# LSH attention with a routed MoE on one core: the mask's store split into the exchange, the bits weighted on ScalarE, and a new order of a pair

## The chip, the cores and the metric

The kernel runs on one core of a Trainium2 chip. The metric is the device time of one execution in microseconds. The core has TensorE (PE in the profile, PEld for its weight loads), VectorE (DVE), ScalarE (ACT), GpSimd (POOL) and SyncE (SP), which here only issues DMAs. Every engine works through its own list of instructions in order and waits for the others through semaphores.

## The reference, cut

Four batches of eight heads with 768 positions of 64 numbers. A query sees a key only where six sign bits of their projections agree. What attention gives goes, token by token, to one of eight experts.

```python
q_bits = (np.einsum('bhsd,dk->bhsk', q, proj) > 0)          # 6 bits of every query, and of every key
mask = q_bucket[:, :, :, None] == k_bucket[:, :, None, :]
scores = np.where(mask, scale * np.matmul(q, k.transpose(0, 1, 3, 2)), -1e9)
attn = np.exp(scores - np.max(scores, -1, keepdims=True))
attn = attn / (np.sum(attn, -1, keepdims=True) + 1e-9)
x = (attn @ v) as rows of one token, all heads side by side  # 3072 x 512
expert_idx = np.argmax(x @ w_gate, axis=1)
y = np.maximum(x @ w1[e], 0.0) @ w2[e]                       # e: the token's expert
out = gate_w[:, None] * y
```

## The kernel before, in words

The attention works on **pairs of heads**: 16 pairs (numbered 0 to 15), four to a batch. A pair has two half pairs (384 queries each) and 12 **score units** of 128 queries by 768 keys of one head. For a unit PE multiplies (`S`, lines 303 and 305: q and k are split into high and low parts, and the low rows also carry the bits of the mask), DVE finds the peak (`R`, L313), two small instructions make the factor and the bias of the exponential (`A`, on the engine whose letter follows: L318 with L322 on POOL or with L320 on DVE), and ACT takes the exponential (`X`, L329). PSUM has three tiles for scores ("s") and two ("t") for everything else.

The weights of the first half pair are turned by PE (`T`, L343) and copied out of PSUM by ACT or DVE (`E`, L369 or L367, "a" or "v"). Those of the second half pair (units 6 to 11) are turned in blocks of 32 by DVE (`D`, L383) and put in their place by the **exchange** (`Y`, L392): 16 stores from one SBUF tile to another, issued by SP once the last turn is done, at the beginning of the next pair. PE multiplies them with v there (`B1-`, L403), ACT copies the result (`O`, L408), PE turns it into token rows and gate logits in one product (`K`, the projection, L422), and DVE scales and stores them (`L`, L432).

The bits of the **next** pair are made inside a pair: `G` (L258, PE, two "t" tiles), `H` (signs, L238, ACT), `w` (L271: the first 64 rows are multiplied by a weight for each row, on POOL; then L272 stores them to DRAM, issued by SP), and `z` (L276): POOL issues a gather from DRAM into the rows of q and k that carry the mask. `C` are the casts and subtractions of the next pair's q and k on POOL (L202 to L210). A pair's x (q and k of a head, 768 KB) is loaded two pairs ahead, v one ahead; both are issued by SP. For pair 15, x is loaded as pair 14 begins.

Once in a batch, in the second pair of the next batch (pairs 5, 9 and 13), the **routing** of the finished batch runs in seven steps (`Z`, lines 454 to 486), mostly on DVE and POOL, and after it six **scatters** (`N`, L497) of token rows to `sorted_rows`, issued by POOL. Before that, eight stores of empty rows (`fill`, L144) must have filled `sorted_rows`.

The order is written out by hand: `HEAD` (pair 0), `NEXT` (pair 1), `PLAN` (pairs 2 to 14) and `LAST` (pair 15) are lists of the letters above, read from left to right, and each engine and each queue gets its instructions in that order. A trailing "-" means the pair before. The loads hang on the scores: `before(c)` runs ahead of units 0, 2, 4, ... (r is c within the pair), and issues x at r = 3 and v at r = 4.

## Time and profile before

| | us |
|---|---|
| median of three runs | 771.81 |
| lowest, highest | 770.47, 773.38 |
| the profiled execution | 770.12 |
| its span, first to last instruction | 768.1 |
| PE busy in it | 729.5 (95%) |
| DVE, ACT, POOL busy | 457.8, 404.5, 513.3 |
| mean granted clock of PE | 0.987 |

The pairs fill the span up to about 450 us, the experts the rest. A row of the timeline has its start in us from the start of the span, how long it lasts, engine, line, operation, tiles written and read, how many instructions it merges, and in brackets how long the engine had been idle before it and what ended that. Tile names are given without their numbers, so `w` can be one of several tiles. The granted clock is 1.00 at 2.4 GHz and 0.50 at 1.2 GHz.

### The profile page before, as it was taken

The numbers are of one execution on the slowest core, as the hardware profiler recorded it, in microseconds if no ns is written. First come the engines' busy times: TensorE is split into PE (matmuls) and PEld (weight loads), VectorE is DVE, ScalarE is ACT, GpSimd is POOL, SyncE is SP. The second block draws the span as 40 slices with busy tenths as digits, with TensorE's granted clock in tenths as the row PEclk, the third lists the DMA queues.
The fourth block names the chain that finished last, engine by engine and source line by source line (L and its number), as shares of the span: only waits on it lengthen the run. The fifth ranks groups of instructions, "written<-read, shape, count | busy, mean of one in ns | idle before, by whom it ended". The sixth has DMA issues, their size and how long they took to land.

```text
span 768.1 us, 13633 instructions
## 1 busy us (share of the span) xinstructions
PE 729.5 (95%) x4675; PEld 584.0 (76%) x4675; DVE 457.8 (60%) x861; ACT 404.5 (53%) x815; POOL 513.3 (67%) x800
## 2 busy tenths in 40 slices
PE   7998899899999899989988999999999999999996
PEld 4766577567756766675665688899999999989895
DVE  6759688788778888877878674222545522232221
ACT  5767476577657665674665652443434343434310
POOL 6848677688877787786877364584656656668432
PEclk9999999999999999999999999999999999999999
DMA  5928998658667856966497535663535465545201
GB/s 198 299 74 216 302 296 214 176 174 242 169 191 204 240 144 190 250 162 191 143 242 184 160 104 184 243 216 98 176 133 184 136 118 191 184 137 203 86 10 37
DMA packets 56966, 136.39 MB, mean 178 GB/s; under 512 B 12211, under 2 KB 16051, under 8 KB 56896
## 3 DMA queue, kind: packets, MB, share of 16 engines
q1 hardware_dynamic: 50064, 119.13, 53.5%
q0 software_dynamic: 6688, 16.35, 6.4%
q8 instruction: 38, 0.62, 0.3%
q14 instruction: 32, 0.26, 0.1%
q10 hardware_dynamic: 144, 0.03, 0.0%
HBM read 76.61 MB, written 26.33 MB: 134 GB/s over the span
## 4 chain that ended last, share of the span: by engine, by line
PE 62%; POOL 7%; issue 7%; DVE 6%; ACT 6%; DMA 6%; SPq 5%; POOLq 0%; ACTq 0%; DVEq 0%; another core or an unknown queue 0%
PE s L747 17%; PE t L403 10%; PE s L784 10%; PE s L804 7%; SPq L392 5%; PE s L303 4%; PE t L343 4%; ACT e L329 4%; PE s L305 4%; DVE m L313 3%; DMA masks<-bits 3%; PE t L422 2%; PE t L709 2%; ACT pt L369 1%; DMA xd<-in_qk_dram 1%
## 5 line engine op out<-in xcount | busy, mean ns | idle before, releaser
L329 ACT ACTIVATE e<-s,m 128x768 f32<-128x768 f32 x192 | 190.2, 992 | 115.0 <-POOL m L322 100.3
L313 DVE TENSOR_REDUCE m<-s 128x1 f32<-128x768 f32 x192 | 179.3, 949 | 42.1 <-PE s L305 36.7
L675 POOL TENSOR_TENSOR w<-raw,w 128x512 fp32r<-128x512 f32 x112 | 142.1, 1294 | 45.8 <-ACT w L674 45.2
L403 PE MATMUL t<-pt,vt 128*64 128x384 f32 x768 | 130.9, 490 | 0.0
L747 PE MATMUL s<-xh,w 128*128 128x456 f32 (+6 forms) x672 | 126.8, 346 | 0.0
L747 PEld LDWEIGHTS s<-xh,w 128*128 128x128 f32 x672 | 119.2, 188 | 2.9
L343 PE MATMUL t<-ident,e 128*128 128x128 f32 x648 | 93.8, 280 | 9.9 <-ACT pt L369 7.4
L403 PEld LDWEIGHTS t<-pt,vt 128*64 128x64 f32 x768 | 52.3, 137 | 64.9 <-issue 63.7
L343 PEld LDWEIGHTS t<-ident,e 128*128 128x128 f32 x648 | 74.8, 142 | 25.7 <-ACT pt L369 12.8
L383 DVE STREAM_TRANSPOSE w<-e 128x768 f32<-128x768 f32 x84 | 79.1, 961 | 23.4 <-ACT e L329 23.1
L763 DVE SCALAR_TENSOR_TENSOR hh<-s,hh 128x256 fp32r<-128x256 f32 (+7 forms) x64 | 35.5, 555 | 91.2 <-ACT hh L761 87.0
L784 PE MATMUL s<-hh,w 128*128 128x456 f32 (+3 forms) x384 | 78.7, 358 | 0.0
L369 ACT ACTIVATE pt<-t 128x512 f32<-128x512 f32 (+1 forms) x113 | 65.1, 587 | 14.2 <-PE t L343 13.5
L761 ACT ACTIVATE hh<-s 128x256 fp32r<-128x256 f32 (+7 forms) x64 | 31.4, 490 | 76.8 <-PE s L747 76.8
L784 PEld LDWEIGHTS s<-hh,w 128*128 128x128 f32 x384 | 69.9, 188 | 2.4
L817 POOL DMA_INDIRECT out_dram<-y,ix x26 | 25.9, 996 | 67.6 <-DVE y L815 31.6
L674 ACT ACTIVATE w<-raw 128x512 fp32r<-128x512 f32 x112 | 66.3, 623 | 1.7 <-DMA raw<-in_w_dram 1.7
L303 PE MATMUL s<-w 80*128 80x384 f32 x192 | 58.5, 387 | 8.9 <-ACT e L329 5.5
L318 POOL TENSOR_SCALAR m<-m 128x1 f32<-128x1 f32 x126 | 29.5, 234 | 49.2 <-DVE m L313 38.4
L804 PE MATMUL s<-w,hh 128*128 128x512 f32 (+1 forms) x240 | 58.9, 398 | 0.0
L303 PE MATMUL s<-qk 80*128 80x384 f32 x192 | 56.4, 376 | 1.3 <-ACT e L329 0.6
L715 DVE TENSOR_TENSOR xh<-t,xh 128x456 fp32r<-128x456 f32 (+6 forms) x28 | 16.0, 575 | 64.3 <-ACT xh L714 64.0
(211 smaller groups left out, 1117.4 us busy)
## 6 DMA issues: line engine op xcount, KB each, us to landing
raw<-in_w_dram SPq DMA_DIRECT2D x64, 512.0 KB
pt<-w SPq DMA_DIRECT2D x224, 144.0 KB
xd<-in_qk_dram SPq DMA_DIRECT2D x16, 768.0 KB
w<-in_qk_dram SPq DMA_DIRECT2D x14, 768.0 KB
sorted_rows<-xr SPq DMA_DIRECT2D x8, 1156.0 KB
xg<-sorted_rows SPq DMA_DIRECT2D x25, 289.0 KB
vt<-in_v_dram SPq DMA_DIRECT2D x16, 384.0 KB
masks<-bits SPq DMA_DIRECT2D x15, 192.0 KB
```

The source lines that it names most:

```text
L303: nc.tensor.matmul(p[:, a, :HALF], k[0:80, 2, c], k[0:80, 3, n], start=i >= 4, stop=i < 4)
L313: nc.vector.tensor_reduce(m[:, 0:1], p[:, :, :HALF], axis=AX.XY, op=OP.max, negate=True)
L329: nc.scalar.activation(e, p[:, :, :HALF], AF.Exp, bias=m[:, 2:3], scale=m[:, 1:2], accum_out=SM[g, hf][:, t, s:s + 1])
L343: nc.tensor.transpose(p[:, x * 128:(x + 1) * 128], e[w][:, kt // 3, (kt % 3) * 128:(kt % 3) * 128 + 128], ident)
L369: nc.scalar.activation(o, x, AF.Copy)
L383: nc.vector.transpose(d.rearrange("p b k q -> p k b q"), PP.pop(i).rearrange("p a c -> p (a c)"))
L403: nc.tensor.matmul(p[s * 64:(s + 1) * 64, :HALF], VT[g][:, kt, s, :], x, start=(kt == 0), stop=(kt == NT - 1))
L674: nc.scalar.activation(w[:, 0, a], r, AF.Copy)
L675: nc.gpsimd.tensor_tensor(w[:, 1, a], r, w[:, 0, a], op=OP.subtract)
L747: nc.tensor.matmul(p[:, :c], w[:, a, d, fs], x[:, b, d, :c], start=(k == 0), stop=(k == 11))
L784: nc.tensor.matmul(p[:, :c], w[:, a, f % 4, ms], h[b][:, f, :c], start=(k == 0), stop=(k == 23))
L804: nc.tensor.matmul(p[:pw], HH[n][b][:, f, i:i + pw], w[:, a, f % 4], start=(k == 0), stop=(k == 23))
```

## The change

- **Exchange in two parts.** `exchange` takes rows: `Y0-` issues twelve stores as the pair begins, `Y1-` the other four later. The mask's store (`w`) stands between them, ahead of the x loads.
- **The weighting of the bits** (`lsh_bits`) is an activation on ACT with a scale for each row.
- **Loads.** Pair 15's x has tiles of its own (one shares the memory of a tile that serves constants at the start and the experts at the end) and is loaded in pair 13 like the others two pairs ahead. v has two buffers in place of three, and is loaded at r = 5 (in pair 0 at r = 4).
- **Empty rows.** Four stores in pair 0 and four in pair 1, in place of two in each of pairs 0 to 3.
- **A new order of a pair**, in `NEXT` and `PLAN`; in `LAST` only the exchange's two parts and the sums move. `G` stands ahead of the projection `K0-`; the routing's first step stands behind score 4; factors 0, 4 and 5 go to DVE, 7 to POOL; the copies E00, E10 and E12 are DVE's in place of E01, E02 and E20, but in pairs 5, 9 and 13 E00 and E10 are ACT's. Both sums (`M`) stand at the end of the pair.
- **Scatters** stand at two fixed places in the three pairs behind a routing's begin (`N0` in the middle, `N1` at the end); batch 2's last four stand in pair 14.

```diff
     def load_x(h):
         g = h // 2
-        x = room[:, h % 2] if g % 2 and g < NG - 1 else wk.tile([128, 2 * S], F32, name="xd")
+        if g == NG - 1:
+            x = (wk if h % 2 else moe).tile([128, 2 * S], F32, name="xl" if h % 2 else "xhe", bufs=1)
+        else:
+            x = room[:, h % 2] if g % 2 else wk.tile([128, 2 * S], F32, name="xd")
...
-        VT[g] = wk.tile([128, NT, 2, D], F32, name="vt", bufs=3)
+        VT[g] = wk.tile([128, NT, 2, D], F32, name="vt")
...
-        nc.gpsimd.tensor_scalar(r[0:64], r[0:64], wsg[0:64], None, op0=OP.mult)
+        nc.scalar.activation(r[0:64], r[0:64], AF.Copy, scale=wsg[0:64])
         nc.sync.dma_start(md[g], r)
...
-    def exchange(g):
+    def exchange(g, rows):
...
-        for a in range(4):
+        for a in rows:
             for b in range(4):
                 nc.sync.dma_start(PT[u][32 * b:32 * b + 32, a], d[32 * a:32 * a + 32, b])
...
     PLAN = """
-        O0- S0 S1 Y0- C00 C01 C02 K0- Z0 S2 R0 R1 Z1 A0P A1P L0- G C03 C04 R2 X0 Z2 A2V S3 R3 X1 N0 S4 H Z3 A3P X2 Z4
-        R4 Z5 T00 E00a T01 S5 N1 X3 E01v T02 T10 R5 Z6 S6 A4P C05 E02v A5P R6 X4 E10a T11 X5 T12 A6V w M1- E11a S7 N2
+        Y0- S0 R0 O0- S1 S2 C00 C01 C02 A0V X0 G R1 A1P R2 S3 H A2V X1 R3 K0- X2 L0- T00 C03 E00v A3P C04 S4 Z0 T01 S5
+        X3 R4 E01a C05 A4V Z1 R5 A5V T02 T10 w Y1- X4 N2 E02a C06 E10v S6 R6 X5 A6V S7 Z2 C10 Z3 Z4 C11 T11 E11a Z5
...
-            late = {(2, 1): 3, (2, 2): 4, (2, 3): 5} if b == B - 2 else {(2, 3): 3, (3, 0): 4, (3, 3): 5}
-            at = {(1, 3): 0, (1, 4): 1, (2, 0): 2} | late
+            at = {(q, k): 2 * q + k - 2 for q in (1, 2, 3) for k in (0, 1)}
+            if b == B - 2:
+                at |= {(2, 2): 2, (2, 0): 3, (2, 3): 4, (2, 1): 5}
...
-        if r == 3 and g + 2 < NG - 1:
+        if r == 3 and g + 2 < NG:
...
-        if g + 1 < NG and r == 4:
+        if g + 1 < NG and r == (5 if g else 4):
             load_v(g + 1)
-        if g < 4 and r > 3:
-            fill(2 * g + r - 4)
+        if g < 2 and r > 3:
+            fill(4 * g + 2 * r - 8)
+            fill(4 * g + 2 * r - 7)
...
-            trans_ev(6 * n + int(x[0]), int(x[1]), x[2] == "v")
+            trans_ev(6 * n + int(x[0]), int(x[1]), x[2] == "v" and not (n % NP == 1 and n > NP and x in FREE))
...
     for g in range(NG):
-        if g == NG - 2:
-            load_x(2 * g + 2)
-            load_x(2 * g + 3)
```

What the lists do on three engines. SP's queue within one pair and up to the next one's exchange, before (`pt` is the tile that the exchange fills, `w_1985` the tile of the turns, `xd` and `w_69` hold x, `vt` holds v):

```order
L392 DMA pt<-w_1985 32x1152 x16
L76 DMA xd<-in_qk_dram 128x1536 x2
L272 DMA masks<-bits 128x384
L81 DMA vt<-in_v_dram 128x768
L392 DMA pt<-w_2299 32x1152 x16
```

and now (the same tiles have other numbers):

```order
L396 DMA pt<-w_1984 32x1152 x12
L275 DMA masks<-bits 128x384
L396 DMA pt<-w_1984 32x1152 x4
L79 DMA xd<-in_qk_dram 128x1536 x2
L84 DMA vt<-in_v_dram 128x768
```

The mask's store has moved ahead of the two x loads, and four of the sixteen exchange stores stand behind it.

PE near the beginning of a pair, from the projection of the old pair's first half on, before (`s` a score, `t` the other PSUM tiles, `wgt` the projection, `pj` the bits, `ident` the transposes):

```order
L422 MATMUL t<-wgt,ot 128x144 x3
L303 MATMUL s<-qk 128x384 x2
L305 MATMUL s<-qk 128x384 x2
L258 MATMUL t<-w_69,pj 32x192 x16
L303 MATMUL s<-qk 128x384 x2
L305 MATMUL s<-qk 128x384 x2
```

and now, from the third score on:

```order
L306 MATMUL s<-qk 128x384 x2
L308 MATMUL s<-qk 128x384 x2
L261 MATMUL t<-w_69,pj 32x192 x16
L306 MATMUL s<-qk 128x384 x2
L308 MATMUL s<-qk 128x384 x2
L426 MATMUL t<-wgt,ot 128x144 x3
L346 MATMUL t<-ident,e 128x128 x4
```

The bit projection now stands ahead of the projection, with one score between them.

DVE where pair 9, which has the routing, begins, before (L454 to L460 are the routing's reduces):

```order
L432 TENSOR_TENSOR xr<-t,r 128x3x144
L454 TENSOR_REDUCE rl<-xr 128x24 x2
L455 TENSOR_REDUCE rf<-rl 128x6
L313 TENSOR_REDUCE m<-s 128x1 x2
L460 TENSOR_REDUCE rf<-rl 128x6
L432 TENSOR_TENSOR xr<-t,r 128x3x144
```

and now:

```order
L436 TENSOR_TENSOR xr<-t,r 128x3x144
L316 TENSOR_REDUCE m<-s 128x1
L321 TENSOR_SCALAR m<-m 128x1
L323 TENSOR_SCALAR m<-m 128x1
L316 TENSOR_REDUCE m<-s 128x1 x2
L321 TENSOR_SCALAR m<-m 128x1
L323 TENSOR_SCALAR m<-m 128x1
L316 TENSOR_REDUCE m<-s 128x1
L436 TENSOR_TENSOR xr<-t,r 128x3x144
L458 TENSOR_REDUCE rl<-xr 128x24 x2
```

The reduces of the routing have moved behind the first four peaks and behind the second L432 (now L436).

## Rows read from the trace of the kernel before

**Rows 1.** The page: busy time, share of the span, instructions.

```profile
PE 729.5 (95%) x4675; PEld 584.0 (76%) x4675; DVE 457.8 (60%) x861; ACT 404.5 (53%) x815; POOL 513.3 (67%) x800
```

**Rows 2.** Stretches from pair starts: PE, PEld, DVE, ACT, POOL busy; clock; DMA share; GB/s.

```profile
93.64:120.65 27.01, 26.70 (x177) 19.59 (x177) 20.35 (x32) 17.18 (x34) 18.34 (x35) 0.89 0.95 266
120.65:145.34 24.69, 24.37 (x179) 17.35 (x178) 20.68 (x33) 16.95 (x34) 18.35 (x35) 1.00 0.72 193
145.34:172.80 27.46, 25.23 (x186) 17.43 (x185) 22.53 (x43) 17.21 (x35) 20.96 (x44) 1.00 0.68 188
...
249.45:278.20 28.75, 26.35 (x186) 18.73 (x185) 22.99 (x46) 17.22 (x35) 22.95 (x47) 0.94 0.68 186
...
355.90:384.35 28.45, 26.27 (x187) 18.66 (x185) 22.63 (x43) 17.15 (x35) 21.99 (x46) 0.94 0.60 161
...
198.18:213.57 15.39, 14.80 (x122) 12.70 (x120) 13.42 (x26) 11.29 (x23) 14.05 (x26) 1.00 0.83 200
```

**Rows 3.** PE's timeline: pairs 3, 7, 8, 9, 11 and 14.

```profile
93.64 0.98 PE L303 MATMUL s<-w 80*128 80x384 f32 x2 [2.98 <-DMA w<-masks]
...
199.70 0.90 PE L422 MATMUL t<-wgt,ot 128*128 128x144 f32 x6
200.34 0.61 PE L303 MATMUL s<-w 80*128 80x384 f32 x2
...
201.23 1.23 PE L258 MATMUL t<-xd,pj 64*32 64x192 f32 x32
...
213.57 2.16 PE L403 MATMUL t<-pt,vt 128*64 128x384 f32 x12
...
228.17 0.88 PE L258 MATMUL t<-w,pj 64*32 64x192 f32 x30 [0.68 <-DVE xr L432]
...
253.87 0.88 PE L258 MATMUL t<-xd,pj 64*32 64x192 f32 x30 [0.87 <-DVE xr L432]
255.72 0.62 PE L303 MATMUL s<-w 80*128 80x384 f32 x2 [0.97 <-ACT e L329]
...
329.64 1.00 PE L422 MATMUL t<-wgt,ot 128*128 128x144 f32 x6 [1.63 <-ACT ot L408]
...
389.34 0.56 PE L258 MATMUL t<-xd,pj 64*32 64x192 f32 x16 [1.05 <-DMA xd<-in_qk_dram]
...
397.33 1.09 PE L343 MATMUL t<-ident,e 128*128 128x128 f32 x8 [1.79 <-ACT pt L369]
```

**Rows 4.** SP's timeline, pairs 7 and 13: first issue, time for all.

```profile
198.44 12.07 SPq L392 DMA_DIRECT2D pt<-w  x16
210.61 1.02 SPq L76 DMA_DIRECT2D w<-in_qk_dram  x2
211.72 0.38 SPq L272 DMA_DIRECT2D masks<-bits  x1
...
355.06 10.90 SPq L392 DMA_DIRECT2D pt<-w  x16
```

**Rows 5.** POOL's timeline, pair 7: the weighting and the first gather.

```profile
207.34 1.27 POOL L271 TENSOR_SCALAR bits<-bits,wsg 64x384 f32<-64x384 f32 x1
...
220.46 0.62 POOL L276 DMA_DIRECT2D qk<-masks  x1 [4.29 <-DMA masks<-bits]
```

**Rows 6.** ACT's timeline, pair 7: signs, a copy out of PSUM, an exponential.

```profile
202.80 0.73 ACT L238 ACTIVATE bits<-t,small 128x192 f32<-128x192 f32 x2
...
207.47 0.59 ACT L369 ACTIVATE pt<-t 128x512 f32<-128x512 f32 x1
207.95 1.00 ACT L329 ACTIVATE e<-s,m 128x768 f32<-128x768 f32 x1
```

**Rows 7.** ACT's copies from SBUF in pair 0 (L225): shortest, median, longest in ns.

```profile
L225 ACT ACTIVATE qk<-xd x6: 506/516/528, 4.1 to 8.4; 128x384 fp32r<-128x384 f32 x5, 80x384 fp32r<-80x384 f32 x1
```

**Rows 8.** The tile of the masks, all of its DMAs.

```profile
DMA to landing us min/median/max: 2.6/3.0/7.7
```

**Rows 9.** A stretch in pair 13, columns as in rows 2.

```profile
368.00:369.00 1.00, 0.86 (x6) 0.53 (x4) 0.97 (x5) 1.00 (x3) 0.57 (x3) 1.00 0.00 0
```

More of the change, by code (lines that the diff above doesn't have):

```diff
@@ L105, in iota @@
     def iota(shape, pattern, name, base=0, cm=0):
-        i = const.tile(shape, I32, name=name + "_i")
+        i = moe.tile(shape, I32, name="xhe") if name == "jp" else const.tile(shape, I32, name=name + "_i")
         nc.gpsimd.iota(i, pattern=pattern, base=base, channel_multiplier=cm)
@@ L383, in turn @@
         nc.vector.transpose(d.rearrange("p b k q -> p k b q"), PP.pop(i).rearrange("p a c -> p (a c)"))
-    def exchange(g):
+    def exchange(g, rows):
         u = 2 * g + 1
-        PT[u] = wk.tile([128, 4, 6, NT, 32], F32, name="pt")
-        d = DT.pop(g)
-        for a in range(4):
+        if u not in PT:
+            PT[u] = wk.tile([128, 4, 6, NT, 32], F32, name="pt")
+        d = DT[g]
+        for a in rows:
             for b in range(4):
@@ L410, in sums @@
     def sums(u):
-        r = wk.tile([128, 3, 2], F32, name="r")
+        r = wk.tile([128, 3, 2], F32, name="r", bufs=3)
         nc.vector.tensor_scalar(r, SM.pop(divmod(u, 2)), 1e-9, None, op0=OP.add)
@@ L855, in lsh_attention_moe @@
     NC = NU // 2
+    FREE = ("00v", "10v")
     routes, parts, pick = {}, list(range(16)), pick_first()
@@ L904, in lsh_attention_moe @@
+        R2 S3 H A2V X1 R3 X2 V1- T00 C03 E00v A3P C04 S4 O1- M1- T01 S5 X3 R4 E01a C05 A4V R5 A5V T02 T10 w X4 E02a
+        C06 E10v S6 R6 X5 A6V S7 C10 C11 T11 E11a T12 S8 E12v K1- L1- T20 X6 R7 T21 S9 E20a E21a A7P z0 R8 A8P C12 X7
+        T22 R9 A9P X8 E22a D6 S10 D7 S11 C13 D8 X9 B00 R10 C14 z1 A10P R11 A11P B01 C15 D9 X10 X11 C16 D10 D11 M0 M1
     """.split()
     PLAN = """
-        O0- S0 S1 Y0- C00 C01 C02 K0- Z0 S2 R0 R1 Z1 A0P A1P L0- G C03 C04 R2 X0 Z2 A2V S3 R3 X1 N0 S4 H Z3 A3P X2 Z4
@@ L911, in lsh_attention_moe @@
+        T12 S8 E12v T20 X6 R7 T21 S9 Z6 E20a N0 E21a A7P z0 R8 A8P C12 X7 T22 R9 A9P X8 E22a B10- D6 S10 D7 S11 C13 D8
+        B11- X9 B00 R10 C14 z1 A10P R11 A11P B01 C15 D9 X10 X11 N3 O1- C16 K1- N1 D10 D11 M0 M1 L1-
     """.split()
     LAST = """
-        O0- Y0- S0 K0- R0 L0- S1 X0 R1 S2 S3 R2 X1 X2 S4 T00 T01 R3 E00a E01a R4 S5 X3 R5 T02 X4 X5 E02v T10 S6 E10a
-        T11 T12 E11a R6 S7 T20 S8 R7 E12a T21 X6 S9 E20v X7 E21v B10- B11- O1- M0 R8 T22 E22a x0 R9 X8 T30 X9 g0 V0
-        M1- E30a x2 h0 O0 T31 S10 g2 E31a T40 T32 h2 R10 E40a S11 T41 R11 E32a K0 E41v nA m0 L0 r0 X10 T42 X11 nA E42a
+        Y0- S0 O0- R0 K0- S1 L0- X0 Y1- R1 S2 S3 R2 X1 X2 S4 T00 T01 R3 E00a E01a R4 S5 X3 R5 T02 X4 X5 E02v T10 S6
@@ L917, in lsh_attention_moe @@
+        E10a T11 T12 E11a R6 S7 T20 S8 R7 E12a T21 X6 S9 E20v X7 E21v B10- B11- O1- M0 R8 T22 E22a x0 R9 X8 T30 X9 g0
+        V0 E30a x2 h0 O0 T31 S10 g2 E31a T40 T32 h2 R10 E40a S11 T41 R11 E32a K0 E41v nA m0 L0 r0 X10 T42 X11 nA E42a
         T50 M1 tP E50a r0 m1 T51 nA r0 T52 E51a m2 E52a tP tV u0 u1 nP r0 tP u2 r0 r0 nA V1 d0 nP r0 O1 tP d1 K1- K1
@@ L989, in step @@
         elif op == "Y":
-            exchange(n)
+            exchange(n, ((0, 1, 2), (3,))[int(x)])
         elif op == "C":
```

7 lines of the change are left out of this document (1 added, 6 removed).

## The prediction, made before the change was run

> **What bounds the kernel now.** I read the page's engine line first: TensorE (PE) is busy 729.5 of 768.1 us [rows 1], so time can only come from PE's idle stretches and from stretches at the lower clock. Next the table by stage, cut where PE starts the first score of a pair (pairs count from 0 to 15, and times "after the pair's start" count from there) [rows 2]. Pair 4 takes 24.69 us with PE busy for 24.37 of them: this is what a pair costs when nothing is late. Pair 3 has PE busy 26.70 us for the same work at a granted clock of 0.89, pair 9 26.35 at 0.94 against pair 5's 25.23 at 1.00, and pair 13 26.27. So the loss over the pairs is idle time plus work done partly at 1.2 instead of 2.4 GHz.
>
> Then PE's own rows with what ended each idle time [rows 3]. Three causes carry nearly all of it. (a) **The mask comes late**: 2.98 us before pair 3's first score, ended by the gather of the masks; 1.63 us in pair 11 before the projection L422, ended by the output copy on ScalarE (ACT). How that hangs together shows in pair 7: SyncE (SP) issues the 16 exchange stores from 198.44 for 12.07 us, then both x loads, then the mask's store at 211.72 [rows 4]; GpSimd (POOL) had weighted the bits by 208.61, but its gather starts at 220.46, after 4.29 us of standing still [rows 5]. All that POOL does behind it, the last two factors above all, waits with it, and ACT's last exponentials and the output copy wait for the factors. (b) **The bit projection L258 waits for VectorE (DVE)**: 0.68 us in pair 8 (pair 12 is the same), 0.87 us in pair 9 and 0.97 us more at the next score. The projection needs a PSUM tile that L432 frees, and in pairs 5, 9 and 13 the routing's reduces stand ahead of the peaks and of that L432 on DVE, as the order of the section on the change shows; the two rows of pair 9 stand for the three pairs (0.86 or 0.87 and 0.97 in each). (c) **Pair 14**: 1.05 us for x, which is loaded only as the pair begins, and 1.79 us because the factors stand on POOL behind scatters [rows 3].
>
> **The change, part by part.** *Mask's store.* In the new order it stands behind 12 of 16 exchange stores and ahead of the x loads. 12 stores are 12/16 of 12.07 us, 9.1 us from the exchange's begin [rows 4], and the exchange begins when the pair before has done its last turn. The weighting goes to ACT; the trace does not show it there. The nearest row is ACT's copy from SBUF of 128x384, 0.52 us [rows 7]; POOL's 1.27 us [rows 5] is the other end. I take 0.52, since the free size and the engine are the same. Its place: PE reaches the end of the bit projection after S0, S1, S2 and L258. In pair 7 that end lies 4.3 us after the start (201.23 + 1.23 - 198.18), with one projection L422 ahead of it that now stands behind (199.70 to the next start at 200.34, 0.64), so 3.6 [rows 3]. On ACT follow the signs, 0.7, three exponentials of 1.0, one eviction, 0.5 to the next start [rows 6], and the weighting: 3.6 + 0.7 + 3.0 + 0.5 + 0.5, so it ends 8.3 us after the pair's start. The store is issued then, in 0.4 us. The gather stands on POOL behind the factor of score 7. Two scores of 0.9 and five groups of transposes lie between that score and the first L403, which PE reaches after 13.9 us (below), so score 7 ends near 10 and its factor is made between 11.5 and 13, an estimate. The landing of DMAs on the masks took 2.6 to 7.7 us [rows 8]; with the median of 3.0 the mask is there at 11.7. So (a) goes: 2.98 + 1.63 and the slow clock of pair 3 (26.70 - 24.37 = 2.33), **6.9 us**.
>
> A rule stands against the ease of this. The twelve stores ahead are in the same queue. The Trainium skill, "DMA: Bandwidth & Descriptors" (Queues, rings and completion order), says that an engine takes one ring's descriptors in order and that the completion mark lands only after every earlier write of that engine. By that rule the mask can't count as landed before the twelve stores have drained, and where the exchange starts late the 3.0 us would be too little; the first rival below is this case. The 4.29 us that POOL stood behind the x loads agrees with it.
>
> *What the split costs.* The last four exchange stores now stand behind the mask's store on SP, which waits for ACT; queued behind are these four, x and v. Who waits for the four is the first product with the exchanged weights (L403). In pair 7 PE reached it at 213.57 [rows 3], and was busy for 14.80 us from the pair's start to there [rows 2]; less one score (200.34 to 201.23, 0.89 [rows 3]) that now comes behind it, 13.9. Mask 0.4, four stores 4/16 of 12.07 = 3.0, and the drain: in pair 13 SP issued stores from 355.06 for 10.90 us, to 366.0, with nothing behind them [rows 4], and from 368 the DMA engines stood at 0.00 [rows 9], so at most 2.0. From the weighting's end that makes 5.4 us: 8.3 + 5.4 = 13.7, just ahead of 13.9. Cost 0, with next to no cover: what the weighting is later than 8.5, every pair pays. The drain behind four stores may be shorter than behind sixteen, so I keep 0.
>
> *L258 ahead of L422, and the factors.* PE now runs scores 0 to 2, then L258, and the projection of the old half pair only behind score 3. The first factor moves to DVE, so the first exponential needs no POOL. The routing's reduces come behind score 4. All of (b) goes: 2 x 0.68 + 3 x (0.87 + 0.97) = 6.9, and the clock of pairs 9 and 13, 1.1 + 1.0 = 2.1: 9.0. In these three pairs the two evictions given to ACT instead of DVE cost 0.5 each, and the routing's own steps stand on DVE in the middle of the pair. Bounds 0 and 1.84 a pair (what it loses now); I take 1.1. **9.0 - 3.3 = 5.7 us.**
>
> *x for pair 15* has its own tiles and is loaded a pair earlier, and four of the middle factors leave POOL: (c), **2.8 us**.
>
> *Empty rows*: eight stores of 512 x 578 numbers, 1.18 MB each, in pairs 0 and 1 instead of 0 to 3. In pair 1 that is 4.7 MB plus 2.0 of x and v; at 266 GB/s, what the DMA engines moved in pair 3 at a share of 0.95 [rows 2], 25 us. They begin with the mask some 8 us into a pair of about 30, so the exchange of pair 2 finds up to 3 us of them ahead of it. Bounds 0 and 3; **minus 1 us**.
>
> *The rest of the order* (scatters at two fixed places, sums, v's third buffer gone): v's load now waits for PE to finish with the older v, with nothing behind it on SP but the next exchange, which starts later anyway: 0. The short waits of 0.3 us that most pairs have now may go or be replaced: 0, bounds minus 0.3 and plus 0.4 a pair over 13 pairs.
>
> Sum: 6.9 + 5.7 + 2.8 - 1.0 = 14.4 us. The profiled execution took 770.12 us, 0.2% under the median of 771.81; 770.1 - 14.4 = 755.7. With all bounds at their good end the gain is 6.9 + 9.0 + 2.8 + 3.9 = 22.6 (748), at their bad end 6.9 + 3.5 + 2.8 - 3 - 5.2 = 5 (765).
>
> **The rivals.** *The mask is still late.* With the 7.7 us of [rows 8] it lands at 16.4, 3 us after POOL wants it, and the factors for scores that PE needs stand behind the gather. For: pair 7's exchange began 0.26 us after the pair's start [rows 4], so that twelve stores and their drain reach to 0.3 + 9.1 + 2.0 = 11.4 us. Against: no x is ahead any more. Half of (a) comes back and about 0.5 us in each of 13 pairs is lost: 14.4 - 3.5 - 6.5, about 766.
>
> *ACT becomes the bound.* Up to the first L403, ACT has from 3.6 us on signs, six exponentials, five evictions and the weighting: 0.7 + 6.0 + 2.5 + 0.5 = 9.7 by [rows 6, 7], so 13.3 against PE's 13.9. 0.6 us of waits for factors is all it can take. For: DVE now has five factors and the evictions too. With 0.8 us a pair too much, 13 x 0.8 = 10.4 are given back: 766. The new order then moves waits and removes few.
>
> *Slower: the tail of the exchange.* If the weighting ends later than 8.5 us, the four stores land after PE wants them, and 13 pairs pay each microsecond. At 9.6 the gain of 14.4 is gone; at 10 the kernel is 5 us slower. For: in pair 7 the weighting on POOL ended 10.4 us after the start [rows 5]; as late on ACT, it would give 1.9 us in 13 pairs, 25 us, and 781. Against: it no longer stands behind POOL's subtractions, and in most pairs only four ACT instructions after the signs lie ahead.
>
> **How the numbers follow.** The measurement can tell 0.5%, 3.9 us, from no change. Forecast 0.62 (748 to 764). Mask still late 0.14 (762 to 770; 0.10 faster, 0.04 same). ACT the bound 0.14 (762 to 771; 0.08 faster, 0.06 same). Tail of the exchange 0.10 (0.03 same, 0.07 slower, to 785). Faster 0.80, same 0.13, slower 0.07. The range goes from the good end, 748, to 768: it leaves out about 0.2.
>
> **What would show it.** Right: no idle time of PE ended by masks, by L432 ahead of the bit projection, or by x; pairs of 24.5 to 25 us, and 26 with routing; the weighting on ACT under 0.6 us; the granted clock at 1.00 in pairs 3, 9 and 13. Wrong: waits of PE at the first L403 of each pair (the tail), ACT busy without a gap with PE waiting for evictions (the bound), POOL's gather still behind a mask's landing, or idle time in pair 2 ended by the exchange.

## The result, and the profile after

The changed kernel took 762.14 us (median of 4 runs, 760.56 to 764.62) against 772.44 us for the kernel before beside it: ratio 0.9873, 95% interval 0.9839 to 0.9907, so 10.3 us less, with an interval of 7 to 12 us. The forecast was 755.7 us with a range of 748 to 768: the direction was right and the time is inside the range, 6 us above the point. The profiled execution spans 758.8 us, against 768.1 before.

Numbers in brackets such as [rows 1] name the rows of the kernel before that a row here is to be compared with. Lines of the changed kernel stand three or four further down: the scores are L306 and L308, the transposes L346, the product with the exchanged weights L407 (L403 before). The page, busy time and share of the span of each engine [rows 1]:

```profile
span 758.8 us, 13625 instructions
PE 721.7 (95%) x4675; PEld 582.1 (77%) x4675; DVE 466.6 (61%) x911; ACT 413.3 (54%) x836; POOL 484.7 (64%) x729
```

PE is busy for 7.8 us less, and its idle time has shrunk by only 1.5 us. TensorE worked at the 1.2 GHz level (granted clock 0.5) for as long as before, 17 us over the pairs; part of what went are waits that lie inside a group of instructions and count as busy. The bit projection of 32 matmuls, for one, runs in 0.88 us where it took 1.23 us [rows 3]; in exchange PE now stands idle for 0.5 us ahead of score 3 in nearly every pair, until the first exponential has freed a tile for scores. By pairs, stretches cut at each pair's first score: length, busy time of PE, PEld, DVE, ACT and POOL, granted clock, DMA share, GB/s. The lines are pairs 0, 2, 4, 5, 6, 7 and 14 [rows 2]:

```profile
7.00:36.56 29.56, 27.36 (x171) 19.10 (x171) 20.45 (x45) 20.95 (x45) 23.02 (x29) 0.83 0.72 244
66.85:96.55 29.70, 25.50 (x176) 18.14 (x177) 22.58 (x42) 17.92 (x38) 19.11 (x34) 0.94 0.88 263
121.43:145.88 24.45, 23.84 (x180) 17.27 (x178) 21.32 (x37) 17.32 (x35) 16.38 (x30) 1.00 0.69 191
145.88:172.66 26.78, 24.67 (x186) 17.32 (x185) 22.52 (x45) 18.34 (x38) 18.52 (x38) 1.00 0.65 181
172.66:197.12 24.46, 23.84 (x179) 17.27 (x178) 21.31 (x37) 17.33 (x35) 19.63 (x37) 1.00 0.84 224
197.12:223.34 26.22, 23.88 (x179) 17.43 (x178) 21.52 (x37) 17.34 (x35) 19.31 (x35) 1.00 0.76 210
375.43:403.79 28.36, 25.46 (x180) 18.61 (x178) 25.09 (x45) 17.26 (x35) 20.07 (x39) 0.94 0.60 159
```

Pairs 4 and 6 stand for seven pairs of 24.4 to 24.9 us at full clock (3, 4, 6, 8, 10, 11 and 12): all but pair 3, with 24.88, are better than the best pair before (24.69). Pairs 2, 7 and 14 and the routing pairs (5; 9 and 13 are alike with 26.89 and 27.27) hold what went wrong. The sum by stretches: pairs 3 to 13 took 290.7 us before (93.64 to 384.35 [rows 2]) and take 278.9 now, 11.8 less; pairs 0 to 2 went from 86.7 to 89.6, 2.9 more; pair 14 from 29.1 to 28.4; the rest is 0.4 longer.

PE's timeline, with the idle time ahead of a row in square brackets and what ended it: pair 2 (first two rows), pair 4's score 3 and its first product with the exchanged weights, pair 5, pair 7, pair 14 [rows 3]:

```profile
70.10 0.59 PE L306 MATMUL s<-qk 80*128 80x384 f32 x2 [2.30 <-DMA qk<-masks]
...
86.17 1.19 PE L407 MATMUL t<-pt,vt 128*64 128x384 f32 x6 [1.77 <-DMA pt<-w]
...
125.15 0.62 PE L306 MATMUL s<-qk 80*128 80x384 f32 x2 [0.51 <-ACT e L332]
...
135.47 1.51 PE L407 MATMUL t<-pt,vt 128*64 128x384 f32 x8
...
163.89 0.62 PE L306 MATMUL s<-w 80*128 80x384 f32 x2 [0.96 <-ACT e L332]
...
212.96 0.54 PE L407 MATMUL t<-pt,vt 128*64 128x384 f32 x2 [1.70 <-DMA pt<-w]
...
388.64 0.69 PE L346 MATMUL t<-ident,e 128*128 128x128 f32 x2 [2.25 <-DVE pt L370]
```

SP's timeline, pair 1 (the mask's store and four fills, L147) and pair 4 (twelve exchange stores, mask, four stores, x) [rows 4]:

```profile
52.52 0.34 SPq L275 DMA_DIRECT2D masks<-bits  x1
...
53.88 1.27 SPq L147 DMA_DIRECT2D sorted_rows<-xr  x2
...
55.91 1.47 SPq L147 DMA_DIRECT2D sorted_rows<-xr  x2
...
119.09 7.65 SPq L396 DMA_DIRECT2D pt<-w  x12
129.97 0.33 SPq L275 DMA_DIRECT2D masks<-bits  x1
130.34 2.42 SPq L396 DMA_DIRECT2D pt<-w  x4
132.86 1.03 SPq L79 DMA_DIRECT2D xd<-in_qk_dram  x2
```

ACT's timeline: the weighting in pair 4, and an exponential in pair 5 that waits for a factor on POOL [rows 6]. Then POOL's [rows 5]: both gathers of pair 1, the first gather of pair 2 and that of pair 4, and the first scatter of pair 5:

```profile
129.34 0.61 ACT L274 ACTIVATE bits<-bits,wsg 64x384 f32<-64x384 f32 x1
...
162.76 0.99 ACT L332 ACTIVATE e<-s,m 128x768 f32<-128x768 f32 x1 [2.37 <-POOL m L325]
```

```profile
59.17 0.58 POOL L279 DMA_DIRECT2D qk<-masks  x1
...
63.76 0.56 POOL L279 DMA_DIRECT2D qk<-masks  x1 [0.29 <-POOL qk L211]
...
84.36 0.57 POOL L279 DMA_DIRECT2D w<-masks  x1 [0.50 <-DMA masks<-bits]
...
135.02 0.57 POOL L279 DMA_DIRECT2D w<-masks  x1
...
160.99 1.13 POOL L501 DMA_INDIRECT sorted_rows<-xr,slot  x1 [2.27 <-issue]
```

In pair 4 the weighting starts 7.9 us after the pair's start and the mask's store goes out at 8.5; POOL takes the gather up at 13.6 and finds the mask there; PE reaches L407 at 14.0 and finds the exchanged weights there.

### The profile page after: what moved, and what is told of

Its sections match the earlier page's. It is cut to its first block, busy times and chain, and to the rows that moved or that the text cites. A ratio compares the mean times of both kernels' runs of the same rounds, so it can differ in the third digit from the quotient of the medians.

```text
span 758.8 us, 13625 instructions
## 1 busy us (share of the span) xinstructions
PE 721.7 (95%) x4675; PEld 582.1 (77%) x4675; DVE 466.6 (61%) x911; ACT 413.3 (54%) x836; POOL 484.7 (64%) x729
## 4 chain that ended last, share of the span: by engine, by line
PE 65%; DVE 8%; issue 7%; ACT 6%; POOL 6%; DMA 4%; SPq 2%; POOLq 0%; DVEq 0%; ACTq 0%; another core or an unknown queue 0%
PE s L751 17%; PE t L407 12%; PE s L788 10%; PE s L808 7%; PE s L306 5%; DVE m L316 5%; ACT e L332 4%; PE s L308 4%; PE t L346 4%; DMA pt<-w 3%; SPq L396 2%; PE t L713 2%; PE t L426 2%; ACT pt L372 1%; DVE w L386 1%
## 5 line engine op out<-in xcount | busy, mean ns | idle before, releaser
L407 PE MATMUL t<-pt,vt 128*64 128x384 f32 x768 | 130.9, 490 | 3.6 <-DMA pt<-w 3.5
L407 PEld LDWEIGHTS t<-pt,vt 128*64 128x64 f32 x768 | 53.0, 137 | 66.9 <-issue 62.8
L346 PE MATMUL t<-ident,e 128*128 128x128 f32 x648 | 93.8, 277 | 5.3 <-DVE pt L370 2.5
L346 PEld LDWEIGHTS t<-ident,e 128*128 128x128 f32 x648 | 76.0, 142 | 15.9 <-ACT pt L372 5.2
L321 POOL TENSOR_SCALAR m<-m 128x1 f32<-128x1 f32 x98 | 22.9, 234 | 89.6 <-DVE m L316 86.8
L372 ACT ACTIVATE pt<-t 128x512 f32<-128x512 f32 (+1 forms) x119 | 67.1, 588 | 6.9 <-PE t L346 6.1
L306 PE MATMUL s<-w 80*128 80x384 f32 x192 | 56.7, 376 | 11.4 <-ACT e L332 10.9
L306 PE MATMUL s<-qk 80*128 80x384 f32 x192 | 58.0, 385 | 6.9 <-ACT e L332 3.1
```

The lines of the kernel that those rows point to most:

```text
L306: nc.tensor.matmul(p[:, a, :HALF], k[0:80, 2, c], k[0:80, 3, n], start=i >= 4, stop=i < 4)
L346: nc.tensor.transpose(p[:, x * 128:(x + 1) * 128], e[w][:, kt // 3, (kt % 3) * 128:(kt % 3) * 128 + 128], ident)
L372: nc.scalar.activation(o, x, AF.Copy)
L407: nc.tensor.matmul(p[s * 64:(s + 1) * 64, :HALF], VT[g][:, kt, s, :], x, start=(kt == 0), stop=(kt == NT - 1))
```

## The experiments

The versions were run in three groups, each on one chip and beside the kernel before, whose medians were 771.74, 771.11 and 773.85 us. Ratios go against these.

### The changed kernel again

> The changed kernel once more, to see which of its idle times come back. Measured 762.1 us (span 758.8 in its profile). If the idle times have causes in the order, the same ones return: 2.3 us at the first scores of pair 2, 1.8 us at its first L407, 2.25 us in pair 14 behind three DVE instructions on key (1.77, 0.73, 0.73 us), about 1.2 us in each of pairs 5, 9 and 13 at scores 10 and 11. Rival: some are chance. I expect that the 1.70 us at the first L407 of pair 7 and the 10.2 us of slow clock in the first 20 us are of that kind: then they are not there, and the span is 2 to 5 us shorter.

763.31 us, ratio 0.9883 (0.9851 to 0.9916). The versions of the same group (empty rows, expert choice, undivided exchange) are held against this. The idle times came back, those that were expected to be chance among them: pair 7 waits 2.08 us at its first L407, the clock stands at 0.5 for 10.2 us in pair 0, and the span is 761.5 us, not shorter. Pair 0, whose order the change leaves alone, is a source of scatter: it took 27.7 us where TensorE's granted clock stood at 0.5 for 3.4 us of it, and 30.7 to 31.0 us where it did so for 13.7 us. In the profile after it cost 1.9 us more than in the profile before.

### The x loads alone, in the kernel before

```
-        if r == 3 and g + 2 < NG - 1:
+        if r == (4 if g > 1 else 3) and g + 2 < NG - 1:
             load_x(2 * g + 4)
             load_x(2 * g + 5)
```

> The kernel before with one edit: the two loads of x rows go out one step later, behind the mask's store instead of ahead of it, from the second pair on. All else, the undivided exchange ahead of the mask and GpSimd's weighting among it, stays. Theory of the prediction's first term: the mask was late in pairs 3, 7 and 11 because these loads stood ahead of its store; the waits of 2.98, 0.68 and 1.63 us for masks shrink to nothing or nearly so and the slow clock of pair 3 goes with them, 4 to 7.5 us in all, 764 to 768 us. Rival: the exchange's stores ahead of the mask keep it late whatever stands behind, so that the waits stay, and the time is within 1.5 us of the kernel before, 770 to 773 us; the division of the exchange would then be what the first term needs.

763.54 us, ratio 0.9894 (0.985 to 0.9938), 7.6 us below the kernel before, a slightly larger gain than was expected, and no slower than the whole change as far as the intervals tell. POOL's idle time ahead of the DMAs on the masks, by what ended it (us, times), from the view of the masks' tile: the line for the mask's store of the kernel before, the same of the changed kernel (3.3 of it in pair 0), and all lines of this version, in which that one is missing:

```profile
  DMA masks<-bits: 12.3, 3
```

```profile
  DMA masks<-bits: 3.8, 2
```

```profile
  DVE w L383: 1.0, 2
  issue: 0.9, 3
  POOL w L190: 0.6, 2
```

POOL stood 12.3 us behind the mask's landing and stands there no more, although all sixteen exchange stores are still ahead of the mask's store and POOL still weights the bits. The rival (the exchange keeps the mask late) is out. More than (a) went: pairs 8 and 12 now take 24.68 and 24.67 us instead of 25.52, and the wait of L258 for L432 in them is gone with L258 and L432 where they were. The timeline shows how that wait hung on the mask. DVE in the kernel before, the last turn of pair 7, whose exponential came late behind the gather of [rows 5]; then PE's bit projection of pair 8 in this version:

```profile
222.79 0.98 DVE L383 STREAM_TRANSPOSE w<-e 128x768 f32<-128x768 f32 x1 [3.43 <-ACT e L329]
```

```profile
226.94 1.23 PE L258 MATMUL t<-w,pj 64*32 64x192 f32 x32
```

DVE came out of pair 7 late and so was late with L432; the 0.68 us of [rows 3] were the mask's, several links further on. In the routing pairs it is otherwise. Pair 5 of this version:

```profile
149.28 0.88 PE L258 MATMUL t<-xd,pj 64*32 64x192 f32 x30 [0.86 <-DVE xr L432]
151.13 0.62 PE L303 MATMUL s<-w 80*128 80x384 f32 x2 [0.97 <-ACT e L329]
```

The two waits are as long as before, and pairs 9 and 13 have them too (0.85 or 0.86, and 0.97): these are not the mask's.

### The last pair's x a pair earlier, on top of that

```
-        VT[g] = wk.tile([128, NT, 2, D], F32, name="vt", bufs=3)
+        VT[g] = wk.tile([128, NT, 2, D], F32, name="vt")
...
+        if g == NG - 1:
+            x = (wk if h % 2 else moe).tile([128, 2 * S], F32, name="xl" if h % 2 else "xhe", bufs=1)
...
-        if r == (4 if g > 1 else 3) and g + 2 < NG - 1:
+        if r == (4 if g > 1 else 3) and g + 2 < NG:
```

> The kernel before with the x loads behind the mask's store, as in the version that took 763.54 us, and one more piece of the change: the x rows of the last pair have tiles of their own and are loaded a pair earlier (and v goes out a step later, with two buffers). Theory of the prediction's third term: the wait of pair 14 for x (1.66 us there) goes, and what follows in pair 14, factors late on GpSimd, takes part of it back: 1 to 2 us less, 761.5 to 762.5 us. Rival: the factors on GpSimd end pair 14 whatever x does, and the time stays at 763 to 764.5 us. Second rival: v's two buffers make products wait for v; then pairs grow by 0.3 us or more and the time is above 765 us.

761.52 us, ratio 0.9862 (0.9819 to 0.9905). The intervals of the two overlap, so 2.0 us is no shown gain; in the profile pair 14 falls from 29.25 to 28.41 us, the wait for x (1.66 us) is gone, and the wait of 1.79 us for factors in pair 14 stays. v's two buffers cost nothing that can be seen: pairs 8 and 12 take 24.67 and 24.68 us. So two small edits, with the order, GpSimd's weighting and the undivided exchange of before, reach the time of the whole change as far as the intervals tell.

### ScalarE's weighting and the division of the exchange

Three versions of the changed kernel: the bits weighted on GpSimd; the exchange undivided, the mask's store behind all of it; both.

```
-        nc.scalar.activation(r[0:64], r[0:64], AF.Copy, scale=wsg[0:64])
+        nc.gpsimd.tensor_scalar(r[0:64], r[0:64], wsg[0:64], None, op0=OP.mult)
```

> The changed kernel with the bits weighted on GpSimd again, and nothing else: one instruction of the mask changes its engine, every other instruction keeps its place. Theory of the prediction: the mask's store and what stands behind it on the DMA queue, the last part of the exchange, go out as much later as the weighting takes longer on GpSimd (1.27 us beside some 0.6 us on ScalarE, and what GpSimd has ahead of it); with the exchange's tail reached by the first product that reads it at about the time at which it lands, that product waits some 0.5 to 0.8 us in each of about 13 pairs, and the time is 7 to 10 us above the changed kernel, 769 to 773 us. Rival: mask and tail have more room than that, ScalarE only passes the 0.6 us on, and the time stays within 1.5 us of the changed kernel, 761 to 764 us.

```
-            exchange(n, ((0, 1, 2), (3,))[int(x)])
+            exchange(n, ((0, 1, 2, 3), ())[int(x)])
```

> The changed kernel with all sixteen exchange stores ahead of the mask's store (the exchange not divided; the mask's store still ahead of the x loads). Theory A: the division is not needed, since the exchange now starts 1 to 2.5 us before the pair and is issued by 8.5 to 9.5 us; the mask's store goes out 0 to 1.5 us later and still lands before POOL wants it at 13.6, while the exchange ends 2 us earlier, so that the waits at the first L407 (pairs 2 and 7, 1.8 and 1.7 us) shrink: 758.5 to 762. Theory B: the division is what brings the mask in time; undivided, POOL's gather waits for its landing in most pairs, and the time grows by 3 to 10 us to 765 to 772.

> The changed kernel with the exchange undivided ahead of the mask's store and the bits weighted on GpSimd. With the division, the weighting on GpSimd cost 7.2 us (the changed kernel of 762.14 us became 769.33 us), since four exchange stores stood behind it. Theory: without the division nothing that TensorE wants soon stands behind the weighting; the mask's store goes out at 9.6 us after a pair's start or when the 16 exchange stores are issued (8.1 to 11.1 us), and the gathers at 14 to 15.5 us are met as with ScalarE; 759 to 763 us, within 1.5 us of the 760.55 us that the undivided exchange gave with ScalarE's weighting. Rival: GpSimd's 0.7 us more stands ahead of its factors, and each pair pays it whatever the exchange does: 767 to 771 us.

Weighted on GpSimd: 769.33 us, ratio 0.9978 (0.9949 to 1.0007), the gain of the change gone. Undivided: 760.55 us, 0.9852 (0.9818 to 0.9885). Both: 761.38 us, 0.9859 (0.9808 to 0.991). So ScalarE's weighting is worth 7 us, but only because the division put four exchange stores behind it, and the division itself brings nothing that can be seen. SP in pair 4 of the version weighted on GpSimd, and PE's first product with the exchanged weights there:

```profile
134.33 0.33 SPq L275 DMA_DIRECT2D masks<-bits  x1
134.71 2.42 SPq L396 DMA_DIRECT2D pt<-w  x4
```

```profile
139.57 1.83 PE L407 MATMUL t<-pt,vt 128*64 128x384 f32 x10 [0.82 <-ACT e L332]
```

The mask's store goes out 9.6 us after the pair's start (124.73), 1.06 us later than in the changed kernel. The last store is issued by 137.13, and PE goes on 2.44 us after that. In the changed kernel the issue ends at 130.34 + 2.42 = 132.76; 2.44 us more is 135.20, and PE comes to L407 at 135.47: the cover was 0.27 us. 1.06 less 0.27 is 0.79, and 0.82 is what PE waits. The cover is an estimate. The changed kernel's second profile, which has landings for these stores, gives some 0.3 us too: pair 4's last store lands at 137.21, PE goes on 0.24 us behind the landing in pair 7, where it waits, and it comes to L407 of pair 4 at 137.76. (The releaser named in the row, an exponential, is the event that came last by the profile; in the changed kernel L407 runs while that exponential is still going, and in pair 3 of this version the same wait of 0.84 us is put down to `pt<-w`.)

With the exchange undivided pair 7's wait is gone too: PE's L407 there, pair 7 of that version, 24.44 us long against 26.22:

```profile
212.10 1.83 PE L407 MATMUL t<-pt,vt 128*64 128x384 f32 x10
```

In exchange the gathers wait for the mask in seven pairs from pair 2 on, longest in pairs 2, 10 and 11 (1.5 to 1.9 us; pairs 10 and 11 take 24.97 and 25.46 us).

### The change in the order of before

The tables and scatter places of before, with the rest of the change: the four stores right behind the mask's, x behind it.

```
-        Y0- S0 R0 O0- S1 S2 C00 C01 C02 A0V X0 G R1 A1P
+        O0- S0 S1 Y0- C00 C01 C02 K0- Z0 S2 R0 R1 Z1 A0P
...
+        X4 E10a T11 X5 T12 A6V w Y1- M1- E11a S7 N2
...
-        if r == 3 and g + 2 < NG:
+        if r == (4 if g > 1 else 3) and g + 2 < NG:
```

> The changed kernel with the order of the kernel before: tables and scatter places of before, the divided exchange with its last four stores behind the mask's, x behind the mask, ScalarE's weighting, the tiles and the empty rows of the change. Theory: the division needs the new order. In the old order ScalarE reaches the weighting only behind the sixth exponential, about 11.2 us after a pair's start, so the last four stores go out from 12.4 to 15 us and land at about 16.6 us, against 15.0 to 15.4 us at which the first product with the exchanged weights is reached; 1.2 to 1.7 us of wait in ten pairs without routing, 774 to 781 us. Rival: the order brings little of its own; the time stays within 3 us of the changed kernel, 760 to 765 us.

797.73 us, ratio 1.0328 (1.0279 to 1.0377), 24 us slower than the kernel before; more than expected. Pair 4 of this version, from 126.59: ACT's weighting, SP's four stores, PE's first product:

```profile
136.92 0.62 ACT L274 ACTIVATE bits<-bits,wsg 64x384 f32<-64x384 f32 x1
```

```profile
137.94 2.41 SPq L396 DMA_DIRECT2D pt<-w  x4
```

```profile
142.81 2.16 PE L407 MATMUL t<-pt,vt 128*64 128x384 f32 x12 [1.18 <-ACT e L332]
```

The weighting starts 10.3 us after the pair's start, the issue ends at 140.35, and 2.44 us later, at 142.79, the tail is there: the same rule gives the 1.18 us. What was not expected is the routing pairs: there the weighting comes at 14.5 us, pairs 5, 9 and 13 take 31.2 to 33.1 us, and the pairs behind them 27.6 to 29.3. The version with the last pair's x a pair earlier has the same order and tiles and takes 761.52 us; what differs between the two is the division with ScalarE's weighting, and the empty rows. The division needs both ScalarE and the new order, to break even.

### The empty rows

```
-        if g < 2 and r > 3:
-            fill(4 * g + 2 * r - 8)
-            fill(4 * g + 2 * r - 7)
+        if g < 4 and r > 3:
+            fill(2 * g + r - 4)
```

> The changed kernel with the stores of empty rows two in each of pairs 0 to 3, as before. Theory: the four stores of pair 1 (4.7 MB) lie ahead of the exchange of pair 2 and of the mask's gathers for it; without two of them the gathers land in time, the exchange's data end 5 us or more earlier, pair 2 falls from 29.7 to about 25, and the time from 762 to 756 to 758. Rival: pair 2 waits because its exchange is divided and its weighting late (11.3 us after its start); then the wait at the first L407 stays at 1.5 us or more and the time within 1.5 us of the changed kernel.

759.42 us, ratio 0.9837 (0.9796 to 0.9879), 3.9 us below the changed kernel beside it, with overlapping intervals, and above the 756 to 758 that were expected. In the profiles pair 2 falls from 31.06 us (with the clock at 0.5 for 6.8 us) to 26.91 (with none), and its wait at L407 from 2.01 to 0.71 us; pair 3, which now has fills, grows from 24.89 to 25.40. The exchange of pair 2, issued over 15.8 us in the changed kernel (68.00 to 83.77), takes 12.8. What the fills do to pair 2 is shown; how much of the median it makes is known to some 4 us only.

### The expert choice in pair 14

```
-            if g == NG - 2 and w in ("R5", "R7", "R9", "S11"):
+            if g == NG - 2 and w in ("A0V", "R7", "R9", "S11"):
```

> The changed kernel with the first step of the expert's choice in pair 14 (three DVE instructions on 8 numbers a partition) moved from behind peak 5 to behind factor 0, where POOL stands idle. Theory: these three are slow only because POOL is at work on SBUF beside them (each ended when POOL's instruction ended); here they take 0.16 to 0.18 us each, the 2.25 us of PE in pair 14 and the slow clock behind it go, pair 14 falls from 28.4 to 24.6 to 25.5, the time by 3 to 4 us to 758 to 759. Rival: they wait for the routing's result or for something else that goes with them; then they are as long here, pair 14 stays above 27.5, and the time does not fall.

759.77 us, ratio 0.9848 (0.9813 to 0.9883), 3.5 us less, intervals overlapping; pair 14 falls from 27.43 to 25.88 us, and the 2.25 us ahead of L346 are gone. In the changed kernel DVE's three key instructions on 8 numbers a partition, and POOL's beside them:

```profile
384.37 1.77 DVE L518 TENSOR_TENSOR key<-pb,base 128x8 f32<-128x8 f32 x1
386.17 0.73 DVE L520 COPY key_c<-key 128x8 f32<-128x8 f32 x1
386.94 0.73 DVE L521 SCALAR_TENSOR_TENSOR key<-key,desc 128x8 f32<-128x8 f32 x1
```

```profile
383.95 1.10 POOL L501 DMA_INDIRECT sorted_rows<-xr,slot  x1 [0.17 <-issue]
385.08 1.02 POOL L213 TENSOR_TENSOR w<-xhe,w 64x384 fp32r<-64x384 f32 x1
386.04 0.83 POOL L205 CAST w<-xl 128x768 fp32r<-128x768 f32 x1
386.81 0.82 POOL L207 CAST w<-xl 128x768 fp32r<-128x768 f32 x1
```

and DVE with the step at the earlier place:

```profile
377.74 0.15 DVE L518 TENSOR_TENSOR key<-pb,base 128x8 f32<-128x8 f32 x1
377.93 0.17 DVE L520 COPY key_c<-key 128x8 f32<-128x8 f32 x1
378.13 0.17 DVE L521 SCALAR_TENSOR_TENSOR key<-key,desc 128x8 f32<-128x8 f32 x1
```

3.23 us became 0.49. Each of the three long ones ends within 0.05 us of an instruction of POOL (386.14 and 386.10, 386.90 and 386.87, 387.67 and 387.63). That the neighbour matters and not the place, the two versions with the weighting on GpSimd show: the step stands where the change put it, POOL does other work beside it, the three take 0.16, 0.48 and 0.17 us, the wait of 2.25 us is gone, and pair 14 takes 26.44 and 26.13 us.

### The first scatter of the routing pairs, later

```
+    ROUTE = [w for w in PLAN if w != "N0"]
+    ROUTE.insert(ROUTE.index("A8P") + 1, "N0")
```

> The changed kernel with one step moved: in the three pairs that hold a routing block (5, 9 and 13) the first scatter stands behind the factor of score 8 on GpSimd instead of ahead of the factor of score 7. Theory: in the changed kernel these pairs lose 1.2 to 1.4 us each at scores 10 and 11 (0.82 to 0.96 us and 0.21 to 0.49 us of TensorE's idle time), because the scatter waits for the last routing step on VectorE and the factor behind it, and ScalarE's product behind that, come late. With the scatter later these gaps go, pairs 5, 9 and 13 fall from 26.7 to 27.3 us to 25.5 to 26 us, and the kernel is 2.5 to 4 us below the changed kernel, 758.5 to 760.5 us. Rival: VectorE's own routing work is what is late, so that the gaps move to a score's peak; then the three pairs stay at 26.5 us or more and the time within 1.5 us of the changed kernel.

759.5 us, ratio 0.9842 (0.9797 to 0.9886): inside what was expected, but its intervals overlap those of the changed kernel, and the profile says that the reason is not the one given. The gaps at scores 10 and 11 are gone and pairs 5, 9 and 13 take 25.57, 25.39 and 25.72 us. But pairs 6 and 10 grow. Pairs 5 and 6 of this version:

```profile
147.46:173.03 25.57, 24.41 (x187) 17.36 (x185) 21.95 (x43) 18.31 (x38) 17.65 (x37) 1.00 0.68 190
173.03:198.73 25.70, 23.89 (x179) 17.41 (x178) 21.79 (x40) 17.33 (x35) 20.71 (x38) 1.00 0.79 220
```

Together they take 51.27 us; the changed kernel took 26.78 + 24.46 = 51.24 us for them; pairs 9 and 10 took 51.48 and now 51.47. In pair 6 PE waits 1.19 us at L407. DVE's last turn of a routing pair ends 0.16 us before the next pair's start instead of 1.06, so the exchange begins later and its data, the divided tail last, lands 1.2 us later. The time was moved over the pair's border. Only behind pair 13 it is kept (pairs 13 and 14: 55.6 us before the edit, 53.1 with it, of which one stretch of the lower clock is part).

### Several together

Two combinations of the edits above: all four (empty rows, undivided exchange, choice, later scatter), and the empty rows and the choice alone.

> The changed kernel with four edits together: the fills of empty rows two in each of the first four pairs as in the kernel before, the exchange undivided ahead of the mask's store (the x loads still behind it), the first step of the expert choice in pair 14 at an earlier place, and the first scatter of the routing pairs behind the factor of score 8. If the four act in different places, their gains add: 4 us from the fills, 2 to 3.5 us from the choice, 1.5 to 2 us from the undivided exchange, 2.5 to 4 us from the scatter, 749 to 753 us. Rival: the gains of the fills and of the undivided exchange are mostly chance of the first pairs' slow clock, or the edits meet in the same queue; then 755 to 759 us.

> The changed kernel with two edits: the empty rows two in each of the first four pairs, and the first step of the expert choice in pair 14 at an earlier place. Exchange divided and scatters as in the changed kernel. If these two carry the gain of the version with four edits (756.09 us) and the undivided exchange and the later scatter give nothing lasting (pairs 5 and 6 together took 51.2 us with and without the later scatter), this one comes out at 754.5 to 757.5 us. If the undivided exchange or the scatter bring something of their own, it comes out at 758.5 us or more.

All four: 756.09 us, ratio 0.9791 (0.9749 to 0.9832), the best version here. The two: 757.49 us, 0.9812 (0.9767 to 0.9857). The single gains don't add: 749 to 753 was expected of the four if they did, and the rival's 755 to 759 came. The two that act in places of their own carry nearly all; the undivided exchange and the later scatter meet in pairs 6 and 10 (26.54 and 26.02 us), where the exchange begins late and the mask now stands behind all of it.

## Why the prediction came out where it did

Its terms gave 14.4 us; the profiles show 9.3, the medians 10.3. Set against the stretches of the profiles: (a) without the 2.98 us that lay ahead of pair 3's first score, and (b), were 3.96 + 5.7 = 9.7 us over pairs 3 to 13; measured 11.8. Pairs 0 to 2 should have gained those 2.98 less 1.0 for the empty rows; they lost 2.9, which is 4.8 us off. Pair 14 should have gained 2.8 and gained 0.8. The last pair is 0.4 longer. 2.1 - 4.8 - 2.0 - 0.4 is the 5 us by which the profiles fell short. That the time still lies 6 us from the forecast is in part luck: errors of both signs met.

**(a), right, and in the profiles larger than it was put.** The x loads were what made the mask late, and moving them alone gave 7.6 us, with an interval of 5 to 12. With the order of before and the two edits above, pairs 3 to 13 take 282.3 us, 8.4 less than before. The prediction counted the mask's way with twelve stores ahead and ScalarE's weighting; neither was needed. The slow clock of pair 3 and the waits of pairs 7, 8, 11 and 12 went with them.

**(b), its cause right in the routing pairs and wrong in pairs 8 and 12, its size too large.** It was put down to the place of L258 behind L432. With the order of before and the x loads behind, pairs 8 and 12 take 24.7 us, down from 25.52: their wait was the mask's. In pairs 5, 9 and 13 the waits of 0.86 and 0.97 us stay in that version, and 27.46 us with them where the clock stands at 1.00, which is what pair 5 took before; the new order takes these waits away, as the prediction had it. The lower clock of pairs 9 and 13 was gone without the new order, but pair 5 had a stretch of it instead; what moves it is not shown. The new order's own share is 0.24 us in pairs 8 and 12 and 0.2 to 0.7 in the routing pairs. Over pairs 3 to 13 it is, with the rest of the change, 278.9 against 282.3 us, 3.5 us where the term had 5.7, in two profiles that have no lower clock in these pairs. The routing pairs' give-back, 1.1 us each, was well sized (they take 26.8 to 27.3 us; "26 with routing" was too low), but its place is POOL: the scatter of 160.99 waits for routing's last steps and the factor of score 7 stands behind it.

**The division, priced rightly at nothing.** Weighting at 7.9 us and 0.61 us long (0.52 was taken, from [rows 7]), store at 8.5, L407 at 14.04 (13.9 was forecast), the tail's landing 0.27 us ahead of it (0.2 was forecast). Two errors cancel in that: the four stores took 2.42 us to issue and not 3.0, and PE could go on 2.44 us behind them and not 2.0. "What the weighting is later than 8.5, every pair pays" is what the version weighted on GpSimd shows, 7 us for 1.06 us. The rival with the slow tail, at 0.10, was near: the old order gives it, 797.7 us. Where the prediction fell short is pair 7, with 1.70 us at L407: the drain was taken as at most 2.0 us behind the last issue; PE went on 2.44 us behind it in pair 4's case above, and 3.7 us in pair 7 (209.23 to 212.96). SP also took longer to issue pair 7's four stores, 3.16 us against 2.42 in pair 11, which has the same scatters and no such wait:

```profile
206.07 3.16 SPq L396 DMA_DIRECT2D pt<-w  x4
```

The profile counts one transfer of instructions (0.02 MB) between 205 and 214 us and none beside pair 11's four stores. The wait of pair 7 comes back in every version with the new order, the divided exchange and ScalarE's weighting (1.10 to 2.08 us, the four issued in 2.95 to 3.25 us), each time with such a transfer beside the four. With the undivided exchange it is gone. In the version weighted on GpSimd the transfer starts 0.8 us ahead of the four, these take 2.42 us, and pair 7 waits no more than its neighbours (0.97 us; 1.08 and 0.83); there pair 9 has one beside its four stores, which take 2.88 us, and it waits 1.96 us where pairs 5 and 13 wait 1.45. So that transfer is the likely cause; no run was made to move it alone. ACT as a bound did not come, but for the 0.5 us ahead of score 3.

**Empty rows, mis-sized.** The term was 1 us with bounds of 0 and 3, reached by counting what is left ahead of pair 2's exchange. It named the right cause and missed the first victim. The four fills of pair 1 go out from 53.88. POOL finds the mask there at 59.17, but the first gather of pair 1 then lands only 7.6 us after its issue, and PE can go on with the second one's rows 6.3 us after its issue (63.76 to 70.10), where the second gathers of later pairs land in 2.7 to 3.4 us. PE waits 0.40 and 2.30 us for the two at pair 2's start. Then comes the exchange, with 1.77 us at its tail. By the versions with the fills in two and in four pairs it is 3.9 us in the medians, known to some 4 us. Of the 4.8 us in pairs 0 to 2, 1.9 are pair 0's clock in the two profiled executions, and no work of the change.

A rule named in the prediction bears on this. The Trainium skill, "DMA: Bandwidth & Descriptors" (Queues, rings and completion order), lets a transfer count as done only when what its engines took before it is written. The trace agrees: the mask's store of [rows 4], behind sixteen stores and two loads, was issued at 211.72 and let the gather go at 220.46, 8.7 us later [rows 5]; in pair 2 of the changed kernel, behind twelve stores, 79.74 to 84.36, 4.6 us. The landings of 2.6 to 7.7 us that the prediction took from [rows 8] for the mask's store are the gathers' alone, since that trace has no landing for this store. The second profile of the changed kernel has them, here for the mask's fifteen stores:

```profile
DMA to landing us min/median/max: 1.9/1.9/4.5
```

The 4.5 is pair 2's, 3.3 is pair 7's. So 3.0 was the price of another transfer, more than most pairs need and too little in these two. With all sixteen stores right ahead of the mask's (the undivided exchange) it is 2.8 to 4.6 us. The rule did no harm because POOL wants the mask at 13.6 us after the pair's start and not at 11.5 to 13, and the store goes out at 8.5. The first rival's price, 7.7 us, came from the same misreading.

**Pair 14, mis-sized.** The wait for x went, as (c) had it, and POOL's factors no longer stop PE. A cost that had no row before came in: the key instructions of the expert choice, 3.23 us instead of 0.50, and behind them 2.25 us of idle PE. In the profile after, the clock stood at 0.5 for 3.4 us from 388.3 on, at the end of that wait; in the second profile the same wait came without it, and pair 14 took 27.43 us. It could have been read from the order: the step's place in the new table lies where POOL has a subtraction and two casts in a row.

## What to carry to other kernels

Ask of each wait what made the engine late that is named in its row, and price the first link alone: here one step's shift of two loads gave, as far as the intervals tell, as much as the whole change, and in two pairs waits put down to a PSUM tile went with it. A store that is split around another store makes the second half as late as whatever the middle one waits for; before that is done, look for who is queued behind, and for how much cover the reader at the end has (some 0.3 us here). What is saved in one pair must be looked for in the next before it is counted.

## What was not expected of the hardware

Three DVE instructions on 8 numbers a partition took 1.77, 0.73 and 0.73 us beside GpSimd instructions, and 0.15, 0.17 and 0.17 us without them. The Trainium skill, "SBUF — State Buffer" (Who interferes with whom), states the rule that fits: VectorE's second pair of SBUF ports is GpSimd's only one, an instruction of VectorE with two inputs in SBUF, or a copy in a two-port mode, and one of GpSimd that reads SBUF exclude each other, and the later one waits for the whole of the other. The trace agrees: each of the three ends where one of POOL's ends. One row does not fit: in the version weighted on GpSimd the copy ends with that weighting (395.64 and 395.62 us), but the first of the three, with two inputs in SBUF, runs in 0.16 us while the weighting is recorded as under way. The 192 peaks of the kernel, which read PSUM, stay between 0.92 and 0.96 us, whatever POOL does beside them.

TensorE's granted clock stood at 0.5, the 1.2 GHz level, for 3.4, 6.8, 10.2 or 13.7 us in pair 0 with the same order there, and that pair took 27.7 to 31.0 us in these executions (in one more, with 32.2 us, the record of the clock begins only at 24 us). It fell at 8.2 to 9.8 us, among the first scores, or at 13.8 to 14.4 us, during or just behind 2 us in which PE stood idle inside the bit projection. No experiment was made on what decides it.
